# One core, decode attention with a gated FFN: the last row of `wo` in loads of 108 and 20 partitions, and hinted rounds on VectorE and ScalarE

## The chip, the cores and the metric

The kernel runs on one core of a Trainium2 chip. The metric is the device time of one execution in microseconds; the median of several runs is compared. A traced execution gives the profile.

## The reference

Two branches read the same `x` (two batches, one token, 640 values) and are mixed by a gate. All is float32.

```python
# B=2, D=640, H=32, Sk=4096, Dh=128, F=1728
q = (x @ wq).reshape(B, 1, H, Dh).transpose(0, 2, 1, 3)
p = softmax(einsum("bhqd,bhkd->bhqk", q, k_cache) * Dh**-0.5)
a = einsum("bhqk,bhkd->bhqd", p, v_cache).transpose(0, 2, 1, 3).reshape(B, 1, H * Dh) @ wo
b = silu(x @ w1) @ w2
g = sigmoid((x * gate_w).sum(-1))
return g * a + (1 - g) * b
```

`k_cache` and `v_cache` hold 134 MB each, `wq` and `wo` 10.5 MB each, `w1` and `w2` 4.4 MB each.

## The kernel before

**Staging.** On-chip memory holds three slabs of 128 partitions x 16,384 floats, 8.4 MB each: `v`, `a` and `b`. First come `w1`, `w2` and `wq` for the FFN and the queries. Then 16 items follow (`items`: groups of four heads, for each batch). Item `i` loads a slab of keys into `a` or `b` in turn, and a slab of values into `v`; the values of the last item go into `a`. All loads are issued by SyncE from one helper (L72), so they stand on one queue in program order; each is spread over sixteen hardware queues.

**One item.** GpSimd multiplies columns 68 to 127 of the key slab by the query, VectorE columns 0 to 67 (`products`) and sums both (`scores`), then finds the maximum (`peak`). ScalarE takes the exponentials (`weights`). TensorE sums them (`total`), makes the next query (`query`), multiplies by the values (`values`) and gathers four heads (`gather`); VectorE scales (`combine`) and turns the result into place in `oP` (`turn`). Step `i` handles the products and scores of item `i` and the values of item `i - 1`. `load_v` and `load_k` of later items wait until the slab is read.

**How the order is written.** `Flow` records each operation with what it reads and writes; `plan` finds the semaphore waits. Then each engine's list is written out: `run` writes it as it stands, `repeat` and `climb` write a loop over equal rounds (TensorE: one item; VectorE: two items, from step 2 on), and `once` writes a stretch as the body of a loop that runs one time: a jump to the body, a branch hint at its head, a register raised by one, and a conditional branch back that is not taken. Before the change `once` is used for one stretch, TensorE's last: all of the output projection.

**The output projection.** `wo` has 4,096 rows, in four groups of 1,024 (`NP` = 4). In a group, partition `p` holds eight rows of 640 floats side by side (`PR` = 8); in what follows "row k" of a group is the k-th of these eight, 128 partitions of 2,560 B. Groups 0 to 2 go into slab `v` after the last values are read from it, group 3 into slab `b`. Groups 0 and 1 are one load, group 2 is two loads of half the columns, group 3 three loads: rows 0 to 4, rows 5 and 6, row 7.

`in_halves` multiplies groups 0 to 2 into a PSUM bank `early`, each row in two halves of the columns with 32 output partitions. Rows below `PACED` go in turn to partitions 0 to 63 and 64 to 127; those of group 2 all go to 0 to 63. `merge` copies `early` into `partial` (ScalarE) and joins the parts with four matmuls. `in_quarters` adds group 3, row by row in four quarters of the columns, 8 matmul records a row. VectorE copies the result to `ot` (L930), SyncE stores it.

A name such as `part("b", 2)` is a piece of a slab in the dependence tracking, not a tile of its own. `FIRST` = 5, `PD` = 5,120 floats, `D` = 640.

Of the kernel before, what the change touches and what calls it, by code (L numbers as in the profile page):

```python
# [189 lines left out]
def gated_decode(nc, x, kc, vc, wq, wo, w1, w2, gate, out):  # L190
    P = 128
    B, H, SK, DH = kc.shape
    D = x.shape[2]
# [18 lines left out]
    NP = HQ // 2  # L212
    PR = 2 * Q
    FIRST = 5
    LEAD = HB // 2
    PACED = (NP - 2) * PR
    items = [(2 * n + u, b) for n in range(NP) for b in range(B) for u in range(2)]
    N = len(items)
    LOOPED = N - 1
# [2 lines left out]
    f = Flow(nc)  # L222
    V, S_, T_, G_ = nc.vector, nc.scalar, nc.tensor, nc.gpsimd

    def sb(name, shape, align=32):
        return nc.alloc_sbuf_tensor(name, shape, F32, align_bytes=align)[tuple([slice(None)] * len(shape))]

    def bank(name):
        return nc.alloc_psum_tensor(name, [P, 512], F32)[:, :]
# [4 lines left out]
    slab = {n: slabs[:, k * SLAB : (k + 1) * SLAB] for k, n in enumerate("vba")}  # L234

    def part(n, *ks):
        return [f"{n}.{k}" for k in (ks or range(8))]
# [13 lines left out]
    g = sb("g", [P, NP * B])  # L251
# [24 lines left out]
    ps_q, ps_o, ps_v, ps_acc, ps_t, ps_m, ps_0, ps_1 = (bank(f"ps{i}") for i in range(8))  # L276
# [9 lines left out]
    PD = PR * D  # L286
# [21 lines left out]
    def load_v(i):  # L308
        src = run_of(vflat, i)
        if i < N - 1:  # L310
            v_load[i] = f.dma("SP", slab["v"], src, writes=part("v"), signal=h_v if i < LOOPED else None)
            return
        f.dma("SP", slab["a"], src, writes=part("a"))

    def load_wo(g):

        n, at = ("v", g * PD) if g < NP - 1 else ("b", 0)
        if g == 0:
            src = wo[: 2 * PR * P, :].rearrange("(g p n) d -> p g (n d)", g=2, n=PR)
            to = slab["v"][:, : 2 * PD].rearrange("p (g c) -> p g c", g=2)  # L320
            f.dma("SP", to, src, writes=part("v", 0, 1), after=v_users)
            return
        if g == 1:
            return
        src = wo[g * PR * P : (g + 1) * PR * P, :].rearrange("(p n) d -> p (n d)", n=PR)
        cuts = (0, PD // 2, PD) if g < NP - 1 else (0, FIRST * D, PD - D, PD)
        after = f.users(part(n)) if g == NP - 1 else v_users
        for k, (c0, c1) in enumerate(zip(cuts, cuts[1:])):
            f.dma("SP", slab[n][:, at + c0 : at + c1], src[:, c0:c1], writes=part(n, g % (NP - 1) + k), after=after)

# [8 lines left out]
        writes=part("v", 0),  # L341
# [9 lines left out]
        reads=["ident"],  # L351
        writes=["ident"],
# [12 lines left out]
        reads=["ident"],  # L365
        writes=["block"],
# [6 lines left out]
        reads=["block"],  # L373
        writes=["fold"],
# [4 lines left out]
        reads=["ident"],  # L379
        writes=["sel"],  # L380
# [4 lines left out]
        reads=["ident"],  # L385
        writes=["half"],
# [9 lines left out]
        reads=["sel"],  # L396
        writes=["pick"],
# [4 lines left out]
        reads=["sel"],  # L402
        writes=["own"],
# [4 lines left out]
        reads=["ident"],  # L408
        writes=["side"],
# [6 lines left out]
        reads=["block"],  # L416
        writes=["spread"],
# [4 lines left out]
        reads=["ident"],  # L422
        writes=["mask"],
    )
    f.op("DVE", lambda: V.memset(join, 0.0), writes=["join"])
    for e in range(2):
        ends, at = join[:, e, ::HB], 64 + HB * (1 - e)
# [5 lines left out]
            reads=["ident", "join"],  # L433
            writes=["join"],
        )
        for t in (at, at + 32):
# [3 lines left out]
                reads=["ident", "join"],  # L440
                writes=["join"],
# [10 lines left out]
        reads=["xs0", "xs1"],  # L452
        writes=["xt"],
# [5 lines left out]
        reads=["xt"],  # L459
        writes=["gx"],  # L460
# [7 lines left out]
    for b in range(B):  # L468
        for j in range(J):
            at = xt[:, j, HB * b : HB * b + 1]  # L470
# [11 lines left out]
                reads=part("a") + ["xt"],  # L482
                writes=[f"hsum{b}"],
            )

    def mm_hr():
# [18 lines left out]
        reads=["ones", "gp"],  # L505
        writes=["ps_o"],
# [6 lines left out]
        reads=["ge"],  # L513
        writes=["g"],
# [4 lines left out]
        reads=["g"],  # L519
        writes=["gc"],  # L520
# [7 lines left out]
    for e in range(2):  # L528
# [3 lines left out]
            reads=["ps_v"],  # L532
            writes=[f"spaced{e}"],
# [8 lines left out]
        reads=["he", "gc"],  # L542
        writes=["he"],
    )
    for e in range(2):
# [5 lines left out]
            reads=["he", "turned", "half", "seq"],  # L551
            writes=[f"seq{e}"],
# [27 lines left out]
    def heads(g):  # L580
        return [f"oP{g}{u}{b}" for u in range(2) for b in range(B)]

    def in_halves(g):

        for k in range(PR):
            s_ = g * PR + k

            def fn(k=k, s_=s_):
                to = 64 * (s_ % 2) if s_ < PACED else 0
                for n in range(2):  # L590
                    at = 32 * (k * NP + g) + LEAD // 2 * n
                    last = T_.matmul(  # L592
                        early[to + 32 * n : to + 32 * n + 32, :],
                        oP[:, at : at + 32],
                        slab["v"][:, s_ * D + n * W2 : s_ * D + (n + 1) * W2],
                        start=(s_ == 0),
                        stop=(s_ in (PACED - 1, PACED + PR - 1)),
                    )
                return last

            f.op("PE", fn, reads=part("v", g + (g == NP - 2 and k >= PR // 2)) + heads(g), writes=["ps_acc"])

    def merge():
        f.op("ACT", lambda: S_.copy(partial, early), reads=["ps_acc"], writes=["partial"])
# [73 lines left out]
    for u in range(2):  # L678
        for b in range(B):
# [7 lines left out]
                reads=[f"ps_{u}", "mask"],  # L687
                writes=[f"qall{u}{b}"],
# [15 lines left out]
    def products(i):  # L704
        k = slab[kslab(i)].rearrange("p (c d) -> p c d", d=DH)
        k0, k1 = part(kslab(i), 0), part(kslab(i), 1)
        f.op(
            "POOL",
            lambda: G_.tensor_mul(k[:, CV:, :], k[:, CV:, :], qsb[:, None, :].to_broadcast([P, C - CV, DH])),  # L709
            reads=["qsb"] + k1,  # L710
            writes=k1,
        )
        f.op(
            "DVE",
            lambda: V.tensor_mul(k[:, :CV, :], k[:, :CV, :], ps_q[:, None, :DH].to_broadcast([P, CV, DH])),  # L715
            reads=["ps_q"] + k0,
            writes=k0,
        )
# [66 lines left out]
    def invert(i):  # L785
        f.op("DVE", lambda: V.reciprocal(ps_t[:, 1:2], ps_t[:, :1]), reads=["ps_t"], writes=["ps_t1"])
        f.op(
            "DVE",
            lambda it=0: V.tensor_mul(rg, ps_t[:, 1:2], column(g, i, it)),
            reads=["ps_t", "ps_t1", "g"],  # L790
            writes=["rg"],
            moves=True,
        )

    def values(i, by=(), loop=None):
        v = slab["v" if i < N - 1 else "a"].rearrange("p (g c) -> p g c", g=NG)

        def groups(*_):
            for gr in range(NG):
                q = gr % 4  # L800
                last = T_.matmul(  # L801
                    ps_v[32 * q : 32 * q + 32, :],
                    pz[:, gr, :],
                    v[:, gr, :],
                    start=(gr < 4),
                    stop=(gr >= NG - 4),
                )
            return last

        f.op(  # L810
            "PE",
            groups,
            reads=part("v" if i < N - 1 else "a") + ["pz"],
            writes=["ps_v"],
            by=by,
            loop=loop,
            lower=[(h_v, 16)],
        )
# [66 lines left out]

    steps = []
    for i in range(N + 1):
        j = i - 1  # L890
        loop = j if 0 <= j < LOOPED else None

        def by(what):
            return [ops[what, j]] if loop is not None else ()

        steps.append(len(f.ops["DVE"]))
        if i < N:
            products(i)
        if j >= 0:
            values(j, by=[v_load[j]] if loop is not None else (), loop=loop)  # L900
            invert(j)
        if 1 <= i < N:
            load_v(i)
        if i < N:
            scores(i)
            if i + 2 < N:
                load_k(i + 2)
            peak(i)
            weights(i)
        if i == N - 1:  # L910
            v_users = f.users(part("v"))
            for g_ in range(NP):
                load_wo(g_)
        if j >= 0:
            combine(j)
            gather(j, by=by("combine"), loop=loop)
            turn(j)
        if i < N:
            inner = i if i < LOOPED else None
            total(i, by=[ops["exp", i]] if i < LOOPED else (), loop=inner)  # L920
            if i + 1 < N:
                query(i + 1, by=[ops["exp", i]], loop=inner)
                copy_q(i + 1)
    edges = steps[2 : N + 1 : 2]
    f.alike["DVE"] = [[f.ops["DVE"][a:b] for a, b in zip(edges, edges[1:])]]
    for g_ in range(NP - 1):
        in_halves(g_)
# [20 lines left out]


    f.plan()  # L950
    for e in ("SP", "POOL", "ACT"):
        f.run(e)
    f.run("DVE", f.ops["DVE"][: edges[0]])
    f.climb("DVE", f.alike["DVE"][0])
    f.run("DVE", f.ops["DVE"][edges[-1] :])
    spans = {"PE": (len(f.ops["PE"]) - NP * PR - 1, len(f.ops["PE"]))}
    for e, (a, b) in spans.items():
        ops, at = f.ops[e], 0
        while at < len(ops):
            end = at  # L960
            if at == a:
                f.once(e, ops[a:b])
                at = b
            elif ops[at].loop is None:
# [3 lines left out]
                at = end  # L968
            else:
# [3 lines left out]
                at = end  # L973
# [21 lines left out]
```

## Time and profile before

| | |
|---|---|
| time, median of 3 runs | 695.82 us (695.63 to 695.86) |
| profiled execution | 696.45 us |
| its span, first to last instruction | 694.3 us |
| mean granted TensorE clock | 0.663 |
| VectorE, GpSimd, TensorE busy | 506.9, 265.6, 212.9 us |
| moved by DMA | 298.32 MB, mean 430 GB/s |

In a profile row, `PE` is TensorE, `PEld` its weight loads, `DVE` VectorE, `ACT` ScalarE, `POOL` GpSimd, `SPq` SyncE. A float32 matmul appears as two records and two weight loads. A timeline row gives the start and the length in us, engine, line, operation, result and operands, the number of records, and in brackets the idle time before it and what ended it. A windows row gives the stretch and its length, the busy time of PE, PEld, DVE, ACT and POOL with their records in brackets, the granted clock as a share of the full one, the mean busy share of the sixteen DMA queues, and GB/s. (A window row of one line alone leaves out the engines that have none of it.) In the chain that ended last each row is start, length, and what. DMA rows give the queue and kind, then packets, MB and share; `instruction` is code that an engine's sequencer fetches.

### The profile page before, as it was taken

To read this page: it belongs to the slowest core of one execution; us is meant where nothing else is said; L and a number is where in the kernel's file an instruction comes from. 1 tells how busy PE (TensorE), PEld (TensorE's weight loads), DVE (VectorE), ACT (ScalarE), POOL (GpSimd) and SP (SyncE) were. 2 spreads that over 40 slices of the span, in tenths; PEclk is the share of its full clock that TensorE was granted. 3 is DMA by queue.
4 is the path that set the end of the run, shared out by engine and by line. 5 is a ranking of instruction groups with operands and counts; after the bars stand their busy time and mean duration, and the time that the engine had idled before them with its cause. 6 is when DMAs were issued, how large, how long until landed. Compare 5 with 4: busy or idle time off the path is not lost. (4 is left out here: it accounts for less than half of the span.)

```text
span 694.3 us, 3766 instructions
## 1 busy us (share of the span) xinstructions
PE 212.9 (31%) x1440; PEld 70.8 (10%) x1440; DVE 506.9 (73%) x269; ACT 40.0 (6%) x152; POOL 265.6 (38%) x26
## 2 busy tenths in 40 slices
PE   0074032141331405060412306060503315060657
PEld 0032010010110101010100101010100101010113
DVE  3910958898989697886959596986959595977811
ACT  0001010101010101010010101010000101010000
POOL 1000908191827090815335180906244270907100
PEclk9988556575565757565665757575665757575689
DMA  9999999999999999999999999999999999999997
GB/s 381 431 438 462 427 423 428 423 464 430 427 430 423 453 438 431 427 427 427 461 430 427 430 423 461 434 427 430 423 457 434 430 427 427 427 461 430 427 416 317
DMA packets 6208, 298.32 MB, mean 430 GB/s; under 512 B 672, under 2 KB 700, under 8 KB 956
## 3 DMA queue, kind: packets, MB, share of 16 engines
q1 hardware_dynamic: 6204, 298.27, 99.3%
q8 instruction: 2, 0.03, 0.0%
q14 instruction: 2, 0.02, 0.0%
HBM read 298.26 MB, written 0.01 MB: 430 GB/s over the span
## 5 line engine op out<-in xcount | busy, mean ns | idle before, releaser
L709 POOL TENSOR_TENSOR slabs<-slabs,qsb 128x7680 f32<-128x7680 f32 x16 | 262.4, 16397 | 378.9 <-DMA slabs<-in_A_k_cache_dram 331.0
L725 DVE TENSOR_REDUCE s<-slabs 128x68 f32<-128x8704 f32 (+1 forms) x32 | 276.3, 8676 | 0.0
L801 PE MATMUL ps<-slabs,pz 128*32 128x512 f32 x1024 | 146.0, 734 | 337.6 <-PEq L156 330.7
L715 DVE TENSOR_TENSOR slabs<-slabs,ps 128x8704 f32<-128x8704 f32 x16 | 147.5, 9221 | 105.4 <-DMA slabs<-in_A_k_cache_dram 105.1
L801 PEld LDWEIGHTS ps<-slabs,pz 128*32 128x32 f32 x1024 | 39.7, 132 | 432.6 <-issue 425.7
L754 ACT ACTIVATE pz<-s,nb 32x128 f32<-32x128 f32 x64 | 25.5, 398 | 546.6 <-PE ps L801 390.3
L839 PE MATMUL ps<-osb,pick 128*128 128x512 f32 x32 | 20.4, 724 | 61.9 <-PEq L156 60.9
L823 DVE SCALAR_TENSOR_TENSOR osb<-ps,rg,own 128x512 f32<-128x512 f32 x16 | 12.0, 750 | 22.4 <-PE ps L801 22.3
L854 DVE TENSOR_REDUCE row<-ps 64x128 f32<-64x512 f32 x16 | 10.9, 682 | 23.3 <-PE ps L839 23.3
L775 PE MATMUL ps<-rs,fold 128*128 128x1 f32 x32 | 6.1, 260 | 40.0 <-PEq L156 39.9
L477 DVE SCALAR_TENSOR_TENSOR slabs<-slabs 128x1728 f32<-128x1728 f32 x8 | 16.1, 2018 | 0.3
L489 PE MATMUL ps<-slabs,xz_col 128*32 128x432 f32 x16 | 2.9, 887 | 33.3 <-DVE slabs L477 33.3
L839 PEld LDWEIGHTS ps<-osb,pick 128*128 128x128 f32 x32 | 5.4, 211 | 76.0 <-issue 74.1
L569 PE MATMUL ps<-slabs,seq 128*32 128x320 f32 x54 | 10.6, 559 | 3.7 <-DVE seq L548 3.7
L754 ACT ACTIVATION_READ_ACCUMULATOR pz<-s,nb 32x1 f32 x64 | 11.8, 184 | 0.0
L775 PEld LDWEIGHTS ps<-rs,fold 128*128 128x128 f32 x32 | 5.9, 219 | 53.1 <-issue 52.1
L861 DVE STREAM_TRANSPOSE ps<-row 64x256 f32<-64x256 f32 x16 | 10.3, 641 | 0.6
L644 PE MATMUL ps<-slabs,xz_col 128*32 128x512 f32 x80 | 9.8, 593 | 0.0
L592 PE MATMUL ps<-slabs,oP_xs 128*32 128x320 f32 x96 | 8.8, 434 | 1.3 <-DMA slabs<-in_A_wo_dram 1.3
L930 DVE COPY slabs<-ps 128x160 f32<-128x160 f32 x1 | 0.3, 325 | 12.1 <-PE ps L622 12.1
L654 PE MATMUL ps<-qall,spread 128*128 (+1 forms) x32 | 8.7, 360 | 0.8 <-ACT qall L682 0.8
L451 DVE STREAM_TRANSPOSE slabs<-oP_xs 128x160 f32<-128x160 f32 x1 | 0.5, 461 | 7.8 <-DMA oP_xs<-in_gate_w_dram 7.8
(63 smaller groups left out, 76.1 us busy)
## 6 DMA issues: line engine op xcount, KB each, us to landing
slabs<-in_A_wq_dram SPq DMA_DIRECT2D x1, 10240.0 KB, 44.6
slabs<-in_B_w_dram SPq DMA_DIRECT2D x2, 4320.0 KB, 17.1
slabs<-in_A_wo_dram SPq DMA_DIRECT2D x1, 5120.0 KB, 21.4
slabs<-in_A_wo_dram SPq DMA_DIRECT2D x2, 1280.0 KB, 25.3
slabs<-in_A_wo_dram SPq DMA_DIRECT2D x1, 1600.0 KB, 30.0
slabs<-in_A_wo_dram SPq DMA_DIRECT2D x1, 640.0 KB, 31.0
slabs<-in_A_wo_dram SPq DMA_DIRECT2D x1, 320.0 KB, 31.3
slabs<-in_A_k_cache_dram SPq DMA_DIRECT2D x16, 47.7
```

Source lines behind the costliest of these rows:

```text
L477: lambda b=b, j=j, at=at: V.scalar_tensor_tensor(hsum[:, b, :], w1t[:, j, :], at, hsum[:, b, :], op0=ALU.mult, op1=ALU.add)
L569: last = T_.matmul(early[to : to + 32, :], seq[:, k : k + 2, :].rearrange("p k z -> p (k z)"), slab[n][:, k * HD : (k + 1) * HD], start=(k ...
L709: lambda: G_.tensor_mul(k[:, CV:, :], k[:, CV:, :], qsb[:, None, :].to_broadcast([P, C - CV, DH])),
L715: lambda: V.tensor_mul(k[:, :CV, :], k[:, :CV, :], ps_q[:, None, :DH].to_broadcast([P, CV, DH])),
L725: lambda c0=c0, c1=c1: V.reduce_sum(Ss[i % 2][:, c0:c1], k[:, c0:c1, :], axis=AX.X),
L754: last = S_.activation(pz[lo:hi, :, 4 * q : 4 * q + 4], s[lo:hi].rearrange("p (g c) -> p g c", c=4), AF.Exp, bias=nb[lo:hi], scale=SCALE, ...
L775: lambda *_: T_.matmul(ps_t[:, :1], fold.rearrange("p a q c -> p (a q c)"), rs, start=True, stop=True),
L801: last = T_.matmul(ps_v[32 * q : 32 * q + 32, :], pz[:, gr, :], v[:, gr, :], start=(gr < 4), stop=(gr >= NG - 4),)
L823: lambda: V.scalar_tensor_tensor(osb, ps_v.rearrange("p (c d) -> p c d", d=DH), rg, own[:, :, None].to_broadcast([P, 4, DH]), op0=ALU.mult ...
L839: lambda *_: T_.matmul(ps_o, pick, osb.rearrange("p c d -> p (c d)"), start=True, stop=True),
L854: lambda: V.reduce_sum(row, ps_o[:64].rearrange("p (c d) -> p d c", d=DH), axis=AX.X),
L861: lambda: V.transpose(oT.rearrange("p n (e i) -> p n e i", e=2), twice),
```

## The change

The third group of `wo` (group 2) is one load. Row 7 of group 3 is two loads, of partitions 0 to 107 (`MOST` = 9 x 12) and 108 to 127, on one semaphore that TensorE awaits at 32. Group 2's matmuls go in turn to both halves of the bank, as those of groups 0 and 1 do. `once` also wraps VectorE's step 1 and ScalarE's exponentials of items 4 to 6 with the query copies behind them; lines after the change stand 5 to 9 further down.

```diff
-    PACED = (NP - 2) * PR
+    MOST = 9 * 12
...
-        cuts = (0, PD // 2, PD) if g < NP - 1 else (0, FIRST * D, PD - D, PD)
-        after = f.users(part(n)) if g == NP - 1 else v_users
-        for k, (c0, c1) in enumerate(zip(cuts, cuts[1:])):
-            f.dma("SP", slab[n][:, at + c0 : at + c1], src[:, c0:c1], writes=part(n, g % (NP - 1) + k), after=after)
+        if g < NP - 1:
+            f.dma("SP", slab[n][:, at : at + PD], src, writes=part(n, g), after=v_users)
+            return
+        after, last = f.users(part(n)), f.sem("last_row")
+        for k, (c0, c1) in enumerate(((0, FIRST * D), (FIRST * D, PD - D))):
+            f.dma("SP", slab[n][:, c0:c1], src[:, c0:c1], writes=part(n, k), after=after)
+        c0 = PD - D
+        f.dma("SP", slab[n][:MOST, c0:PD], src[:MOST, c0:], after=after, count=(last, 16))
+        f.dma("SP", slab[n][MOST:, c0:PD], src[MOST:, c0:], writes=part(n, 2), after=after, count=(last, 32))
...
-                to = 64 * (s_ % 2) if s_ < PACED else 0
+                to = 64 * (s_ % 2)
...
-                        stop=(s_ in (PACED - 1, PACED + PR - 1)),
+                        stop=(s_ >= (NP - 1) * PR - 2),
...
-            f.op("PE", fn, reads=part("v", g + (g == NP - 2 and k >= PR // 2)) + heads(g), writes=["ps_acc"])
+            f.op("PE", fn, reads=part("v", g) + heads(g), writes=["ps_acc"])
...
+        turns.append(len(f.ops["ACT"]))
...
-    for e in ("SP", "POOL", "ACT"):
+    for e in ("SP", "POOL"):
         f.run(e)
-    f.run("DVE", f.ops["DVE"][: edges[0]])
+    for e, (a, b) in (("ACT", turns[4:8:3]), ("DVE", steps[1:3])):
+        f.run(e, f.ops[e][:a])
+        f.once(e, f.ops[e][a:b])
+        f.run(e, f.ops[e][b:] if e == "ACT" else ())
```

The end of SyncE's list, the loads of `wo` and the store. Before:

```order
L72 DMA slabs<-in_A_wo_dram 128x2x5120
L72 DMA slabs<-in_A_wo_dram 128x2560 x2
L72 DMA slabs<-in_A_wo_dram 128x3200
L72 DMA slabs<-in_A_wo_dram 128x1280
L72 DMA slabs<-in_A_wo_dram 128x640
L72 DMA out_dram<-slabs 4x2x160
```

After:

```order
L72 DMA slabs<-in_A_wo_dram 128x2x5120
L72 DMA slabs<-in_A_wo_dram 128x5120
L72 DMA slabs<-in_A_wo_dram 128x3200
L72 DMA slabs<-in_A_wo_dram 128x1280
L72 DMA slabs<-in_A_wo_dram 108x640
L72 DMA slabs<-in_A_wo_dram 20x640
L72 DMA out_dram<-slabs 4x2x160
```

Two loads became one, one became two; nothing else moved on this queue.

TensorE's final round, with the semaphores that its first matmuls await (`load_...` is one load's own). Before:

```order
L592 MATMUL ps<-slabs,oP_xs 32x320 [waits load_420]
L592 MATMUL ps<-slabs,oP_xs 32x320 x7
L592 MATMUL ps<-slabs,oP_xs 32x320 [waits load_421]
L592 MATMUL ps<-slabs,oP_xs 32x320 x7
L609 MATMUL ps<-slabs,join 17x160 [waits done_ACT]
```

After:

```order
L597 MATMUL ps<-slabs,oP_xs 32x320 [waits load_420]
L597 MATMUL ps<-slabs,oP_xs 32x320 x15
L614 MATMUL ps<-slabs,join 17x160 [waits done_ACT]
```

Group 2 is awaited once, whole, before any of its sixteen matmuls.

VectorE at the border of step 0 and step 1. Before:

```order
L743 TENSOR_REDUCE nb<-ps 128x1
L715 TENSOR_TENSOR slabs<-slabs,ps 128x8704
L786 RECIPROCAL ps<-ps 128x1
L789 TENSOR_TENSOR rg<-ps,g 128x1
L725 TENSOR_REDUCE s<-slabs 128x68
```

After:

```order
L748 TENSOR_REDUCE nb<-ps 128x1
L141 UNCONDITIONAL_BRANCH
L143 BRANCH_PREFETCH_HINT
L720 TENSOR_TENSOR slabs<-slabs,ps 128x8704
L791 RECIPROCAL ps<-ps 128x1
L794 TENSOR_TENSOR rg<-ps,g 128x1
L730 TENSOR_REDUCE s<-slabs 128x68
```

A jump and a hint stand ahead of step 1; behind it stand an addition and a compare. ScalarE has the same four around its items 4 to 6.

More of the change, by code (lines that the diff above doesn't have):

```diff
@@ L884, in turn @@
         )
-    steps = []
+    steps, turns = [], []
     for i in range(N + 1):
```

## The prediction

> **What bounds the kernel now.** I read the page first, then the chain that ended last, then the DMA queues and the windows of the last two microseconds, and last the timeline of that stage.
>
> ```profile
> span 694.3 us, 3766 instructions
> PE 212.9 (31%) x1440; PEld 70.8 (10%) x1440; DVE 506.9 (73%) x269; ACT 40.0 (6%) x152; POOL 265.6 (38%) x26
> DMA packets 6208, 298.32 MB, mean 430 GB/s; under 512 B 672, under 2 KB 700, under 8 KB 956
> ```
>
> No engine is busy for more than 73% of the span. The 298.32 MB are what fills it:
>
> ```profile
> 300.00:500.00 200.00, 61.45 (x398) 18.71 (x402) 157.19 (x71) 11.12 (x45) 81.93 (x5) 0.64 1.00 435
> 689.90:690.10 0.20, 0.20 (x13) 0.19 (x9) 0.00 (x0) 0.00 (x0) 0.00 (x0) 1.00 0.53 205
> 690.30:690.50 0.20, 0.20 (x12) 0.20 (x8) 0.00 (x0) 0.00 (x0) 0.00 (x0) 1.00 0.28 115
> 690.50:690.70 0.20, 0.20 (x16) 0.19 (x9) 0.00 (x0) 0.00 (x0) 0.00 (x0) 1.00 0.17 64
> 690.90:691.10 0.20, 0.20 (x12) 0.09 (x8) 0.00 (x0) 0.00 (x0) 0.00 (x0) 1.00 0.13 51
> 691.10:691.30 0.20, 0.20 (x11) 0.16 (x13) 0.00 (x0) 0.00 (x0) 0.00 (x0) 1.00 0.13 51
> 691.45:691.75 0.30, 0.30 (x12) 0.00 (x0) 0.00 (x0) 0.00 (x0) 0.00 (x0) 1.00 0.00 0
> ```
>
> In these windows the last three columns are the granted clock, the busy share of the sixteen DMA queues and GB/s. In the middle the share is 1.00 and 435 GB/s flow, so nothing that an engine does there shortens the run unless it starves the queues. At the end the share times 16 is the number of queues that still move data: some 8 at 690.0, 4.5 at 690.4, 2.7 at 690.6, and 2 from 690.9 to 691.3 us. The load of a row is spread evenly, but two queues end about 1.4 us after the first half. The kernel waits for these two.
>
> ```profile
> 659.47 29.95 DMA slabs<-in_A_wo_dram
> 689.42 0.14 issue
> 689.56 2.19 PE ps L622 x56
> 691.75 0.51 PE ps L622 x8
> 692.29 0.33 DVE slabs L930
> ```
>
> The chain agrees: loads of `wo` up to 689.42, then TensorE in the last quarter of the projection, where the last eight records begin only at 691.75. The timeline of the weight loads shows which of its starts are waits:
>
> ```profile
> 689.53 1.25 PEld L622 LDWEIGHTS ps<-slabs,oP_xs 128*17 128x17 f32 x40 [0.53 <-issue]
> 691.01 0.41 PEld L622 LDWEIGHTS ps<-slabs,oP_xs 128*17 128x17 f32 x16 [0.23 <-DMA slabs<-in_A_wo_dram]
> 691.75 0.13 PEld L622 LDWEIGHTS ps<-slabs,oP_xs 128*17 128x17 f32 x8 [0.34 <-DMA slabs<-in_A_wo_dram]
> ```
>
> The 40 are rows 0 to 4 of the last group, the 16 rows 5 and 6, the 8 row 7. Each of the three waits for its own load.
>
> **The change, part by part.** *The last row of `wo`.* One load of 128 partitions becomes two, of 108 and 20. How many queues does each use? The 672 packets under 512 B are completion marks: 45 loads and stores were issued, four of them (x, gate, and two of the result) with four rows in DRAM, and 41 x 16 + 4 x 4 = 672. So a transfer takes only as many of the sixteen queues as share its rows evenly: 108 is 12 x 9 and 20 is 10 x 2. If the smaller sets lie inside the larger, ten queues move 11 rows, two move 9 and four none, where each moved 8. Two queues at 51 GB/s are 25.5 GB/s each, so a row of 2,560 B takes 0.10 us. The four without a share end 8 x 0.10 = 0.80 us sooner, the ten end 0.30 us later.
>
> If the two late queues are among the four, their last work is rows 5 and 6, which landed for the start at 691.01. The others are mostly done by 690.1 to 690.3 and reach 690.6 with three rows more, and 0.3 us pass from the queues' end (0.00 from 691.45) to TensorE's start at 691.75, so row 7 would be there at about 690.9. Then TensorE itself is the limit: 40 records took 1.25 us, 0.031 us each, so sixteen need 0.50 us from 691.01, and with some hundredths for the start of a group, which the 0.13 us of eight alone show, row 7 starts at 691.55 and not 691.75. **That is 0.20 us, not the 0.80 us that the queues save**: rows 5 and 6 still come through the late queues.
>
> [...]
>
> *The hinted rounds.* VectorE's second round and ScalarE's fifth to seventh are wrapped in a branch that is hinted and not taken again. The trace has four fetches of code within the span:
>
> ```profile
> q8 instruction: 1, 0.02, 3.0%
> q8 instruction: 1, 0.02, 2.0%
> q14 instruction: 1, 0.01, 0.6%
> q14 instruction: 1, 0.01, 3.9%
> q1 hardware_dynamic: 3906, 178.66, 98.9%
> ```
>
> The first row is of 54 to 56 us, the next two of 110 to 113, the fourth of 276.5 to 277, the last, with no fetch, of 277 us to the end. The two on q14 fall where VectorE begins the round that is now wrapped and just after ScalarE ended its sixth:
>
> ```profile
> 107.28 9.22 DVE L715 TENSOR_TENSOR slabs<-slabs,ps 128x8704 f32<-128x8704 f32 x1 [11.02 <-DMA slabs<-in_A_k_cache_dram]
> 273.25 0.27 ACT L675 COPY qsb<-ps 128x128 f32<-128x128 f32 x1 [0.86 <-PE ps L654]
> ```
>
> In the last window TensorE runs its final round, 168 matmul records with as many weight loads, behind the same kind of hint, and fetches nothing. So I take it that both q14 fetches go. A fetch takes a turn on one of the busy queues, I assume, and a queue that never idles stays late by it until the end; of the about five queues that still ran at 690.4, two would then be these. I take the last two to be those of q8, with 0.02 MB against 0.01, though no row names a queue; and q8 stays. So this term is **0 us by itself**; it makes room for the three more rows. If a q14 queue stayed late (to 690.9) and took three rows, it would end at 691.2, and row 7 would be ready at 691.5, still before 691.55.
>
> What the wrapping costs: two moves of a register, a jump, a hint, an addition and a compare per engine. ScalarE is hidden:
>
> ```profile
> ACT pz L754 <- PE ps L801: 390.3, 11, 36.7
> slabs<-in_A_k_cache_dram SPq DMA_DIRECT2D x16, 47.7
> slabs<-in_A_v_cache_dram SPq DMA_DIRECT2D x16, 29.4
> ```
>
> It waits for TensorE, up to 36.7 us in a round. VectorE does not idle in its second round, and behind it SyncE waits to issue the next load of `k`. A slab of 8.39 MB at 435 GB/s takes 19.3 us, and a load of `v` lands 29.4 us after its issue, so 10.1 us of its time is spent behind earlier loads, for `k` 28.4 us. A delay below 10 us on the way to an issue starves no queue. Cost 0.
>
> *The third group in one load, and its matmuls in both halves of the bank.*
>
> ```profile
> 679.53 4.18 PEld L592 LDWEIGHTS ps<-slabs,oP_xs 128*32 128x32 f32 x66 [2.10 <-DMA slabs<-in_A_wo_dram]
> 679.53 8.81 PE L592 MATMUL ps<-slabs,oP_xs 128*32 128x320 f32 x96 [1.27 <-DMA slabs<-in_A_wo_dram]
> 683.87 0.12 PEld L592 LDWEIGHTS ps<-slabs,oP_xs 128*32 128x32 f32 x2 [0.15 <-issue]
> 685.75 0.12 PEld L592 LDWEIGHTS ps<-slabs,oP_xs 128*32 128x32 f32 x2 [0.15 <-DMA slabs<-in_A_wo_dram]
> 688.39 0.42 ACT L604 COPY slabs<-ps 128x320 f32<-128x320 f32 x1 [28.27 <-PE ps L592]
> 688.87 0.47 PE L609 MATMUL ps<-slabs,join 128*17 128x160 f32 x8 [0.53 <-ACT slabs L604]
> 679.50:683.90 4.40, 4.37 (x66) 2.13 (x68) 1.00 1.03 438
> ```
>
> With four destinations in turn 66 records took 4.18 us, 0.063 each; with two, 2 records every 0.27 us. Before, the third group ran from 683.87 at the slow pace; now it begins when the whole group is there, at 685.75 at the latest, and its 32 records need 2.0 us at the fast pace, plus some 0.3 us of the last one. It ends by 688.1, before the 688.34 (679.53 + 8.81) of now, after which the copy to `partial` begins. The join then ends by 689.3 again, ahead of 689.53. Cost 0, at most 0.05 us of gain by fewer packets.
>
> **Sum:** -0.20 us. The profiled execution took 696.45 us, 0.63 above the median of 695.82; on its own time that is 696.25, on the median 695.6.
>
> **Rivals.** *The late queues are among those that get more* (the slower side). No row says which queue is late. If one of the two is in the ten, it ends 0.30 us later, at 691.75, row 7 starts at 692.05, and the run takes 696.1; with 9 rows it is 0.10 us and 695.9. It decides as soon as one of the two has a share of more than 8 rows. For it: ten or twelve of sixteen get a share, so a blind draw puts both among the four in about one case in ten. Against it: the four-row transfers' queues and the fetching ones need not be drawn blindly, and q14 would have to go for the ten to have room, which the change does.
>
> *The split does nothing*: 108 rows go to all sixteen, 7 rows in most, and 20 add 2 on ten; the late queues then have 7 to 9 rows, and the time is 695.7 to 695.9. Against it stand the 672 marks.
>
> *A branch fetches.* A jump costs more fetches instead of fewer. One q14 fetch of 0.01 MB at a sixteenth of 435 GB/s is 0.3 us on one queue of those with 11 rows; two of them on a queue that ended at 690.9 give 690.9 + 0.6 + 0.3 = 691.8 and row 7 at 692.1, 0.35 us slower, 696.2. Against it: TensorE's round. [...]
>
> *The clock falls.* TensorE now stands still from about 684.2 to 685.6. At half the clock the third group and the 64 last records take twice as long, about 2 us more before the join and 0.6 of rows 5 to 7; less the slack, 1.5 us, 697.3. It decides if a pause of 1.4 us lowers the clock. Against it: the pause just before 679.53 was 1.27 us for PE, and the window after it has 1.00.
>
> **How the numbers follow.** Forecast (gain of 0.1 to 0.4 us, 695.4 to 695.7) 0.62; late queues with more rows 0.19; split does nothing 0.12; branch fetches 0.04; clock 0.03. The likeliest gives 695.6. The range 695.0 to 696.4 takes in the first three cases, with 0.4 us for the spread of the runs (695.63 to 695.86) and of another chip. 0.2% is 1.39 us, about what a measurement of this kernel tells from no change; only the clock and a long starvation reach it: slower 0.04, faster 0.01, same 0.95.
>
> **What would show it.** Right: row 7's weight loads at once behind those of rows 5 and 6, with no wait for a load; two queues busy at 690.5 and none after about 690.7; no q14 packet in the span; the third group's 32 records in about 2 us from 685.6 on, at a clock of 1.00. Wrong: a share of 0.06 to 0.13 up to 691.7 and row 7 at 692.05; q14 packets at other times; a clock of 0.50 after 684.

## The result, and the profile after

The changed kernel took 696.84 us (median of 22 runs, 696.02 to 698.09) against 695.78 us before (22 runs, 695.52 to 696.10). The ratio is 1.0017, 95% interval 1.0010 to 1.0023: about 1.1 us slower, where 0.2 us faster was forecast. One run of an experiment below, of the rounds alone, took 726.40 us at a granted clock of 1.00, and its ratio leaves it out. The profiled execution took 697.23 us. Its page begins, and counts the packets and the code fetches, as follows:

```profile
span 694.8 us, 3774 instructions
...
DMA packets 6071, 298.33 MB, mean 429 GB/s; under 512 B 662, under 2 KB 690, under 8 KB 946
...
q8 instruction: 2, 0.03, 0.0%
q14 instruction: 3, 0.02, 0.0%
```

Three q14 fetches and not none; before there were two. The 662 packets under 512 B are the completion marks: 672 before, less 16 for the load that is gone, and 12 + 10 instead of 16 for row 7. So the two loads use twelve and ten queues, as the prediction counted.

The chain that ended last, of the changed kernel (start, length, what), has the DMA piece end at 691.57 and TensorE start the rest at 691.62:

```profile
658.33 33.25 DMA slabs<-in_A_wo_dram
691.57 0.04 issue
691.62 1.09 PE ps L627 x24
692.71 0.02 issue
692.73 0.33 DVE slabs L936
```

The timeline of its weight loads, rows 0 to 4, rows 5 and 6, row 7 as before:

```profile
689.51 1.25 PEld L627 LDWEIGHTS ps<-slabs,oP_xs 128*17 128x17 f32 x40 [0.90 <-issue]
691.61 0.41 PEld L627 LDWEIGHTS ps<-slabs,oP_xs 128*17 128x17 f32 x16 [0.86 <-DMA slabs<-in_A_wo_dram]
692.20 0.13 PEld L627 LDWEIGHTS ps<-slabs,oP_xs 128*17 128x17 f32 x8 [0.18 <-DMA slabs<-in_A_wo_dram]
```

Rows 0 to 4 start as before (689.53). Rows 5 and 6, whose load was not touched, come 0.60 us later than the 691.01 of before, and row 7 starts at 692.20 and not 691.75. That is 0.45 us in the trace, where the medians are 1.06 us apart: with 694.8 us the traced execution has one of the shortest spans of the changed kernel's 22 (694.7 to 696.1, median 695.3). What the longer ones add no trace shows.

Why the loads are late can be read from the windows. Their last three columns are clock, busy share of the sixteen DMA queues and GB/s. Share and GB/s count the packets that begin in the window, so GB/s divided by the share is the rate that sixteen busy queues would have. Before:

```profile
689.70:690.10 0.40, 0.40 (x17) 0.39 (x13) 0.00 (x0) 0.00 (x0) 0.00 (x0) 1.00 0.79 314
690.10:690.50 0.40, 0.40 (x20) 0.39 (x12) 0.00 (x0) 0.00 (x0) 0.00 (x0) 1.00 0.33 134
690.50:690.90 0.40, 0.40 (x20) 0.27 (x9) 0.00 (x0) 0.00 (x0) 0.00 (x0) 1.00 0.17 64
```

After:

```profile
689.70:690.10 0.40, 0.40 (x17) 0.39 (x13) 0.00 (x0) 0.00 (x0) 0.00 (x0) 1.00 0.99 294
690.10:690.50 0.40, 0.40 (x21) 0.39 (x13) 0.00 (x0) 0.00 (x0) 0.00 (x0) 1.00 0.46 128
690.50:690.90 0.40, 0.40 (x20) 0.26 (x8) 0.00 (x0) 0.00 (x0) 0.00 (x0) 1.00 0.34 122
690.90:691.30 0.40, 0.19 (x8) 0.00 (x0) 0.00 (x0) 0.00 (x0) 0.00 (x0) 1.00 0.13 45
691.30:691.70 0.40, 0.08 (x4) 0.09 (x8) 0.00 (x0) 0.00 (x0) 0.00 (x0) 1.00 0.10 40
```

Before, the first window gives 314 / 0.79 = 397 GB/s. After, the share is higher (0.99) and less is moved: 294 / 0.99 = 297, then 128 / 0.46 = 278 against 406. From 690.5 on it is 346 to 400 again. So for the 0.8 us from 689.7 on, in which row 7's two loads run beside rows 5 and 6, a busy queue moves about a quarter to a third less.

The trace also holds the duration of each packet. Before, each of the 128 packets of row 7 took 102 ns and each of the 128 of rows 5 and 6 took 196 ns. After, 46 and 10 of them took longer, up to 287 and 374 ns; all of these began between 689.6 and 691.1 us.

### The profile page after: what moved, and what is told of

It reads as the page before. It is cut to its first block, busy times and chain, and to the rows that moved or that the text cites. A ratio compares the mean times of both kernels' runs of the same rounds, so it can differ in the third digit from the quotient of the medians.

```text
span 694.8 us, 3774 instructions
## 1 busy us (share of the span) xinstructions
PE 208.4 (30%) x1440; PEld 69.2 (10%) x1440; DVE 506.5 (73%) x269; ACT 40.0 (6%) x152; POOL 265.7 (38%) x26
## 5 line engine op out<-in xcount | busy, mean ns | idle before, releaser
L806 PE MATMUL ps<-slabs,pz 128*32 128x512 f32 x1024 | 144.5, 728 | 337.7 <-PEq L156 329.7
L597 PE MATMUL ps<-slabs,oP_xs 128*32 128x320 f32 x96 | 6.9, 434 | 2.2 <-DMA slabs<-in_A_wo_dram 2.2
```

The costliest lines, as they stand in the source:

```text
L806: last = T_.matmul(ps_v[32 * q : 32 * q + 32, :], pz[:, gr, :], v[:, gr, :], start=(gr < 4), stop=(gr >= NG - 4),)
```

## The experiments

Differences below are of the medians against the kernel before, run on the same chip with it.

**The last row alone, the rounds alone, the third group alone, and the change without the rounds.** Two theories: S, the split itself costs; F, the fetches that the hints bring cost.

The split alone is before with this:

```diff
...
+        f.dma("SP", slab[n][:MOST, c0:PD], src[:MOST, c0:], after=after, count=(last, 16))
+        f.dma("SP", slab[n][MOST:, c0:PD], src[MOST:, c0:], writes=part(n, 2), after=after, count=(last, 32))
```

> The kernel before with the last row of wo as loads of 108 and 20 partitions, nothing else. Theory S (the split itself costs: queues that run ahead write row 7 where the late queues still write rows 5 and 6, and slow them): 0.4 to 0.8 us slower than before, rows 5 and 6 awaited until about 691.4 to 691.6 as in the changed kernel (691.61). Theory F (the split is fine, and the fetches that the hinted rounds bring are what costs): 0.2 us faster, rows 5 and 6 at 691.0 as before and row 7 right behind them.

It took 696.54 us against 695.97, +0.57 (ratio 1.0005, 0.9996 to 1.0014). Its weight loads:

```profile
691.48 0.41 PEld L630 LDWEIGHTS ps<-slabs,oP_xs 128*17 128x17 f32 x16 [0.82 <-DMA slabs<-in_A_wo_dram]
692.07 0.13 PEld L630 LDWEIGHTS ps<-slabs,oP_xs 128*17 128x17 f32 x8 [0.18 <-DMA slabs<-in_A_wo_dram]
```

Rows 5 and 6 are late as in the changed kernel, with no hinted round in the program: theory S. The time alone would not have shown it, since its interval includes 1; the trace does.

The rounds alone:

```diff
+        f.once(e, f.ops[e][a:b])   # ACT: turns[4:8:3], DVE: steps[1:3]
```

> The kernel before with the two hinted rounds alone. Theory F: q14 fetches still in the span, about 4 us behind each hint, and 0.3 to 1.0 us slower with a wide spread. Theory S: the fetches come too, but they put no queue later than the two that are last already; within 0.1 us of before.

695.81 against 695.97, -0.16 (0.9995, 0.9986 to 1.0005). Page and weight loads:

```profile
q14 instruction: 3, 0.02, 0.0%
...
690.99 0.41 PEld L622 LDWEIGHTS ps<-slabs,oP_xs 128*17 128x17 f32 x16 [0.23 <-DMA slabs<-in_A_wo_dram]
691.73 0.13 PEld L622 LDWEIGHTS ps<-slabs,oP_xs 128*17 128x17 f32 x8 [0.34 <-DMA slabs<-in_A_wo_dram]
```

Three fetches, and an end like that of before. Theory F falls: the fetches are there, and no cost of theirs shows.

The third group in one load:

```diff
-                to = 64 * (s_ % 2) if s_ < PACED else 0
+                to = 64 * (s_ % 2)   # and group 2 in one load
```

> The kernel before with the third group of wo in one load and its matmuls in both halves of the bank. Both theories: within 0.1 us of before; the 32 records in about 2 us from 685.6, as in the changed kernel.

695.69 against 695.97, -0.28 (0.9996, 0.9987 to 1.0005). The interval includes 1: no effect is shown, as both theories expected.

The changed kernel without the rounds:

```diff
-        f.once(e, f.ops[e][a:b])   # both engines run straight on
```

> The changed kernel without the hinted rounds (split and third group in one load). Theory S: 0.4 to 0.8 us slower than before, like the split alone. Theory F: 0.2 us faster than before. If only both together cost (a queue made late by the hint's fetch has 11 rows), within 0.2 us of before.

696.56 against 695.97, +0.59 (1.0007, 0.9998 to 1.0016), the same as the split alone; this interval too includes 1.

**What of the split.** Now theory W (a share that lies in partitions which another queue writes slows both) against N (the number of queues, rows or loads). Two halves of 64 partitions leave each queue its 8 rows:

```diff
-    MOST = 9 * 12
+    MOST = 64
```

> The kernel before with row 7 of the last group as two loads of 64 and 64 partitions: every one of the sixteen queues still moves 8 rows, but each writes other partitions than in a load of 128. Theory W (a share that lies in partitions which other queues write slows both): row 7's packets take well over 0.102 us, rows 5 and 6 are awaited past 691.2, 0.3 to 1 us slower than before. Theory N (the number of rows per queue or of queues is what costs): 8 rows each as before, packets 0.102 us, within 0.1 us of before.

697.09 against 695.77, +1.32 (1.0018, 1.0009 to 1.0027). A window and the weight loads:

```profile
690.50:690.90 0.40, 0.40 (x22) 0.36 (x12) 0.00 (x0) 0.00 (x0) 0.00 (x0) 1.00 0.31 51
...
692.13 0.41 PEld L630 LDWEIGHTS ps<-slabs,oP_xs 128*17 128x17 f32 x16 [1.27 <-DMA slabs<-in_A_wo_dram]
693.15 0.13 PEld L630 LDWEIGHTS ps<-slabs,oP_xs 128*17 128x17 f32 x8 [0.61 <-DMA slabs<-in_A_wo_dram]
```

51 / 0.31 is 165 GB/s, less than half of the 376 (64 / 0.17) of before in the same window. By the counting that the 662 marks bear out, no queue has more or fewer rows than before, and it is worse than 108 and 20. N falls for rows and queues; that it is two loads is left.

Two loads of all partitions, half the columns each:

```diff
-        cuts = ... (0, FIRST * D, PD - D, PD)
+        cuts = ... (0, FIRST * D, PD - D, PD - W2, PD)
```

> The kernel before with row 7 as two loads of 320 columns of all 128 partitions: as many loads as in the changed kernel, but each queue keeps its own partitions. Theory W: no packet slower than the shortest of its size, rows 5 and 6 at 691.0 as before, within 0.15 us of before. Theory N (a further load at the end, or smaller packets, cost): 0.4 us or more slower.

695.76 against 695.89, -0.13 (0.9998, 0.9989 to 1.0007):

```profile
689.70:690.10 0.40, 0.40 (x20) 0.39 (x16) 0.00 (x0) 0.00 (x0) 0.00 (x0) 1.00 0.83 311
...
690.96 0.41 PEld L622 LDWEIGHTS ps<-slabs,oP_xs 128*17 128x17 f32 x16 [0.22 <-DMA slabs<-in_A_wo_dram]
691.74 0.13 PEld L622 LDWEIGHTS ps<-slabs,oP_xs 128*17 128x17 f32 x8 [0.38 <-DMA slabs<-in_A_wo_dram]
```

One load more and packets half as long, and nothing is late. The count of loads is not it.

Half of row 7 left out:

```diff
-        f.dma("SP", slab[n][MOST:, c0:PD], src[MOST:, c0:], ...)   # MOST = 64
```

> The kernel before, but row 7 is loaded for partitions 0 to 63 alone, in one load; the other half of row 7 is left out (what was in the slab stays there). Half the bytes. Theory W (the limit is where the data is written, and 64 partitions have half of these places): packets of row 7 that run at the same time take about 0.2 us, twice the 0.102, and those few on late queues hold up rows 5 and 6 as in the changed kernel. Theory N: 0.102 us each, row 7's load ends 0.4 us sooner than before.

```profile
689.70:690.10 0.40, 0.40 (x20) 0.39 (x15) 0.00 (x0) 0.00 (x0) 0.00 (x0) 1.00 0.43 77
...
691.41 0.68 PEld L629 LDWEIGHTS ps<-slabs,oP_xs 128*17 128x17 f32 x24 [0.73 <-DMA slabs<-in_A_wo_dram]
```

77 / 0.43 is 179 GB/s where before had 397, so packets take about twice as long, and with half the bytes rows 5 and 6 still come 0.40 us later than before. The time was 696.02 against 695.89 (1.0003, 0.9992 to 1.0013). These are theory W's numbers.

The durations of single packets, from the traces, side by side:

| kernel | packets of row 7 | packets of rows 5 and 6 |
|---|---|---|
| before; the rounds alone; the third group alone | all 128 took 102 ns | all 128 took 196 ns |
| row 7 as two halves of the columns | all 256 took 55 ns | all 128 took 196 ns |
| the changed kernel, 108 and 20 partitions | 46 of 128 longer than 102 ns, up to 287 | 10 of 128 longer than 196 ns, up to 374 |
| 64 and 64 partitions | 57 of 128, up to 311 | 11 of 128, up to 534 |
| 64 partitions alone | 17 of 64, up to 286 | 12 of 128, up to 485 |

So it is the dealing out of the partitions that slows packets. A queue that gets other partitions also reads other rows of `wo` in DRAM, and no run here separates the reading from the writing.

**Can the split be put where it does no harm?** Row 0 instead of row 7, two loads ahead of the end:

```diff
+        f.dma("SP", slab[n][:MOST, :D], src[:MOST, :D], after=after, count=(first, 16))
+        f.dma("SP", slab[n][MOST:, :D], src[MOST:, :D], writes=part(n, 3), after=after, count=(first, 32))
```

> The kernel before with row 0 of the last group, the first that is loaded, as loads of 108 and 20 partitions, and the three loads behind it of 128 partitions. Theory W: the packets are slowed 2 to 3 us ahead of the end, where nothing waits; the two late queues keep the 0.8 us that they save, the q14 queue with 11 rows is then last: 0.2 to 0.4 us faster than before. Theory N: the cost stays with the split wherever it is, 0.4 to 0.8 us slower.

697.53 against 695.77, +1.76 (1.0023, 1.0014 to 1.0032): the gain that I expected of theory W did not come, and the cost is more than twice what theory N named. Before, and then with the split of row 0:

```profile
684.00:686.00 2.00, 2.00 (x20) 0.82 (x14) 0.00 (x0) 0.00 (x0) 0.00 (x0) 1.00 1.00 425
686.00:688.00 2.00, 2.00 (x18) 0.82 (x14) 0.00 (x0) 0.00 (x0) 0.00 (x0) 1.00 0.94 401
```

```profile
684.00:686.00 2.00, 2.00 (x16) 0.68 (x12) 0.00 (x0) 0.00 (x0) 0.00 (x0) 1.00 1.07 294
686.00:688.00 2.00, 1.72 (x16) 0.78 (x16) 0.00 (x0) 0.00 (x0) 0.00 (x0) 1.00 0.98 349
...
692.68 0.13 PEld L629 LDWEIGHTS ps<-slabs,oP_xs 128*17 128x17 f32 x8 [0.36 <-DMA slabs<-in_A_wo_dram]
```

The queues are all busy and move 294 and 349 GB/s, against 425 and 401 in these windows before. (131 + 52) GB/s x 2 us is 0.37 MB, or 0.84 us at 435 GB/s, and row 7 comes 0.93 us later. With shares of 0.98 from 688 to 689.4 us and 1.05 from 689.7 to 690.1 the queues had no gap there to make it up in. The traced execution is the fastest of this kernel's runs (696.62 us); what the slower ones add, up to the median's +1.76, no trace shows.

With 126 and 2 partitions:

```diff
-    MOST = 9 * 12
+    MOST = 9 * 14
```

> The same with loads of 126 and 2 partitions: fourteen queues with 9 rows, two with one more, two with none. If the two late queues are the two without a share, 0.4 to 0.6 us faster than before (the q14 queue has 0.1 us more and not 0.3); if one or both of them have a share, they end 0.1 us later and the time is 0 to 0.15 us above before.

697.16 against 695.77, +1.39 (1.0018, 1.0009 to 1.0027): neither of the two expected outcomes. Sparing two queues and not four, by the same counting, does not help either.

**Do the rounds add to the split?**

```diff
-    for e, (a, b) in (("ACT", turns[4:8:3]), ("DVE", steps[1:3])):
+    # one of the two engines only
```

> The changed kernel without ScalarE's hinted round. If the queue that VectorE's hint makes late, with 11 rows, is what lifts the changed kernel (696.84) above the one without both rounds (696.56): 0.8 to 1.1 us above before, and row 7 awaited behind rows 5 and 6 as in the changed kernel. If ScalarE's late fetch (691.3) does it: 0.5 to 0.7 above before, like the kernel without both.

> The changed kernel without VectorE's hinted round, with ScalarE's. If ScalarE's late fetch (690.5 to 691.3) is what lifts the changed kernel above the one without both rounds: q14 fetches at about 112.6, 209.2 and 691, and a median 0.2 to 0.4 us above that of e4_no_rounds, like the changed kernel. If it is VectorE's earlier fetch, or chance: within 0.15 us of e4_no_rounds (0.6 to 0.8 above before).

> The changed kernel again, on the same chip as the kernel without VectorE's hinted round: 0.8 to 1.1 us above before.

Without ScalarE's round: 696.59 against 695.77, +0.82 (1.0012, 1.0003 to 1.0021). Without VectorE's: 696.48 against 695.89, +0.59 (1.0007, 0.9998 to 1.0016). The changed kernel beside it: 696.61, +0.72 (1.0008, 0.9999 to 1.0017), less than the 0.8 to 1.1 expected. The four kernels with the split and none, one or both rounds lie between +0.59 and +0.82 here, and one kernel's runs spread over 1.2 us, so no part of the rounds can be told. The first comparison's +1.06 against +0.72 here is one kernel twice; why it differs is open.

## Why the prediction was wrong, point by point

*What bounds the kernel* was right: the DMA stream, and at the end a few late queues and the waits for rows 5 and 6 and for row 7.

*The step that failed* is "a row of 2,560 B takes 0.10 us. The four without a share end 8 x 0.10 = 0.80 us sooner, the ten end 0.30 us later". It took a queue's rate as its own, however the partitions are dealt out. A load of 128 gives each queue 8 partitions (16 marks a load); in 108, 20 or 64 the shares lie otherwise, and the rate fell to 278 of 406 (108 and 20) and 165 of 376 (64 and 64). So rows 5 and 6, forecast at 691.01, came at 691.61 in a load that the change did not touch, and row 7, forecast at 691.55, came at 692.20: +0.45 us for -0.20. The sign named for being right, row 7 at once behind rows 5 and 6, does appear in four other traces with 108 and 20 partitions (the changed kernel again, without both rounds, without the one, without the other). It is no gain there, since rows 5 and 6 come at 691.39 to 691.94.

Why a busy queue moves less there is not shown. The half row alone, in 64 partitions, moved 179 of 397 GB/s in the window, near the half that theory W named; but no run tells the places that are written from the rows that are read.

*The hinted rounds:* "I take it that both q14 fetches go" was wrong. The rows of the DMA view for 100 to 101.5, 209 to 209.7 and 691.2 to 691.5 us of the changed kernel:

```profile
q14 instruction: 1, 0.01, 1.3%
q14 instruction: 1, 0.01, 2.8%
q14 instruction: 1, 0.01, 6.4%
```

They moved from 110 to 113 and 276.5 to 277 ahead to 4 us behind the two hints (hints at 96.84 and 205.30 us, fetches at 100.85 and 209.30), and a third came at the end with ScalarE's round (two in all without it). The term's price, 0 us, was right as far as it can be told (rounds alone: -0.16, interval including 1). That covers the wrapping too. That a fetch takes a turn on one of the busy queues was my assumption: the three rows show a packet of about 0.31 us each (6.4% of 16 x 0.3 us for the last), and not on which queue.

*The third group* was right in time and price:

```profile
685.57 1.77 PEld L597 LDWEIGHTS ps<-slabs,oP_xs 128*32 128x32 f32 x32 [2.10 <-DMA slabs<-in_A_wo_dram]
688.00 0.43 ACT L609 COPY slabs<-ps 128x320 f32<-128x320 f32 x1 [29.02 <-PE ps L597]
686.00:688.00 2.00, 1.93 (x32) 0.65 (x20) 0.00 (x0) 0.00 (x1) 0.00 (x0) 1.00 0.97 410
```

32 records in 1.77 us (2.0 estimated), the copy at 688.00 (by 688.1), at a clock of 1.00: the rival of the falling clock did not come.

*The rivals.* The slower side that I named, late queues with more rows (696.1), has the sign but not the mechanism: the two loads of 64, with 8 rows counted on each of sixteen queues, are slower still (+1.32 us). Whether the two late queues have a share in the changed kernel no view shows. *The split does nothing* fell with the 662 completion marks: 108 rows did not go to all sixteen queues. The chance of one in ten that both late queues are among the four was a slip: 4/16 x 3/15 is one in twenty.

The range ended at 696.4, since each rival of the split was priced at a full rate per queue; no run of before showed a load that was not of 128 or 4 rows, so the bound for such a packet should have been well above the 0.10 us of before (in the changed kernel the longest took 0.29). The 0.95 for no change of 0.2% came true although the sign forecast did not, and does not speak for the mechanism.

## What to carry to other kernels

Where the DMA stream sets the time, as here, a load of other than all 128 partitions should be priced by how its partitions are dealt to the queues and not only by how many rows a queue gets: with loads of 108 and 20, 64 and 64, or 64 partitions alone, busy queues fell in the slowed windows shown to between 44% (165 of 376 GB/s) and 83% (349 / 0.98 of 401 / 0.94) of their rate, packets of loads that had not changed among them. A late queue seen in the last windows is no reason to deal rows to others by splitting the partitions; with a split by columns all 256 packets of row 7 took 55 ns and all 128 of rows 5 and 6 their 196, and no cost of it shows (-0.13 us). When a window's busy share rises and its GB/s falls, divide GB/s by the share: that shows slowed packets, which a busy share alone hides. Compare windows with packets of like size, since the column split's shorter packets (1,280 B in 55 ns, against 2,560 B in 102) gave 311 / 0.83 = 375 in the window where before had 397.

## What the runs showed of the hardware that was not expected

A round wrapped with a hint at its head did not keep the fetch of code away on VectorE and ScalarE: the trace has three q14 fetches where before had two. They came earlier, about 4 us behind the hint (at 100.85 and 209.30 us), and the third, in the window from 691.2 to 691.5 us, with ScalarE's round. And a load that was slow in mid-stream was paid for at the end: 0.84 us of bytes not moved around 686 us, and 0.93 us at row 7.

No version that I ran is shown to be faster than the kernel before; the third group in one load has the lowest median (695.69, ratio 0.9996, 0.9987 to 1.0005), and its interval includes 1.
